# Clustered attention: second operand of odd heads, turn of the cluster scores and the place of the maxima

## Chip, cores and metric

The kernel runs on one core of one Trainium2 chip. The metric is device time in microseconds (us) of one execution; below 0.2% a difference counts as none.

## What is computed

The program is an attention in which a query only sees the keys of its own cluster, followed by two mixture layers. The change touches the attention alone:

```python
q_n = q / (norm(q) + 1e-06); k_n = ...; c_n = ...       # B=2, H=8, S=768, D=64, 16 clusters
q_assign = argmax(einsum('bhsd,hcd->bhsc', q_n, c_n), -1)
k_assign = argmax(einsum('bhsd,hcd->bhsc', k_n, c_n), -1)
mask = q_assign[:, :, :, None] == k_assign[:, :, None, :]
scores = where(mask, scale * q @ k.T, -1e9)
attn = softmax(scores) @ v
x = relu(attn_tokens @ w_in) ** 2 @ w_out               # first mixture layer
out = sum over e of p[:, e] * (relu(x @ w1[e]) @ w2[e]) # second
```

## The kernel before, in words

**Units.** There are 16 heads (batch by head) of six tiles of 128 queries, so 96 units. The loop over `g` (L1234) works on three units at once: it issues the score products of unit g+2 (`S`, L656) and their row maximum (`M`, L665), the exponential of unit g+1 (`E`, L676), the turns of unit g's probabilities (`T0`, `T1`, L689), which ScalarE rounds (`H0`, `H1`, L694) and VectorE completes by the rest (`L0`, `L1`, L695), and the products with v of the two units before (`P0`, `P1`, L703 and L705). Every large product takes its operands as a rounded part and a rest. The order of these steps is written out by hand in `ORDER`, a line for even and one for odd g, and each engine executes its own instructions in that order:

```python
"S T0 X1 M E T1 R Y1 H0 P0 X2 C H1 L0 L1 C K Y2".split(),        # even g
"S X1 E M T0 T1 Y1 H0 C P1 X2 R L0 H1 C L1 Y2 O K C".split()]    # odd g
```

`X1` and `X2` run the TensorE part of a queued job and `Y1`, `Y2` its way out of PSUM; `R` runs jobs that need no TensorE; `C` takes one entry from the queue `dq`, so that an even g takes up to two and an odd g up to three. An entry `None` only passes one turn of `C`.

**Preparing a pair of heads.** While earlier heads are worked on, the next pair j (heads 2j and 2j+1, first unit u0 = 12j) is prepared by jobs that are placed in units by `AT` and `START`. `trans_slot` (L393) turns q and k at u0-14 to u0-11; its way out writes the rounded part and the rest (`nkh`, `nkl`, `nqh`, `nql`, one buffer each) on GpSimd (L53, L402). `pair_scores` (L478) makes the cluster scores of both heads at u0-11 and u0-10, copied by ScalarE to `ys` (L484). `pair_turn` (L494) turns three 128x128 blocks of `ys` with the fp32 identity at u0-10 and u0-9, once for each half of the tokens; a column group holds, for each of four combinations, two parts of 16 scores, and VectorE adds the two parts on the way out (L499). `pair_ops` finds the first best cluster: `first` is a row maximum on VectorE (L535) and three operations on GpSimd (L524 to L526), `second` another maximum (L539) and four GpSimd operations (L529 to L532) that write the one-hot rows `oh`. `pair_hot` (L551) turns `oh` on TensorE at u0-5; ScalarE copies the result (L556), and `hot_rows` sends it by four DMAs (L568) into the last 16 rows of the operands `q2` and `k2`.

**Other jobs.** `stack` copies parts of the pair's q and k by DMA (L414, L416) into the operands of each head: part 0 makes `k1` (rounded part over rest), part 1 makes `k2`, `q1` and `q2`. For an odd head i they stand at 6i-10 and 6i-9; for the pair's numbering, at u0-4 and u0-3. `norm_steps` places the finishing of the pair that is two before: at u0-6 of the pair j its `f4` runs in `R`, two additions of 128x384 on GpSimd (L786), and at u0-5 `f5`, which multiplies and rounds (L740, L749).

Of the kernel before, what the change touches and what calls it, by code (L numbers as in the profile page):

```python
# [8 lines left out]
F32 = mybir.dt.float32  # L9
# [3 lines left out]
ALU = mybir.AluOpType  # L13
AX = mybir.AxisListType
# [11 lines left out]
    "S X1 E M T0 T1 Y1 H0 C P1 X2 R L0 H1 C L1 Y2 O K C".split()]  # L26
WARM = [11, 6, 4, 3, 1, 2]
START = {'t': [0, 0, 1], 'a': [3, 3, 4, 4, 7], 'stack1': 4, 'stack': 5, 'head': 2}
AT = {"stack1": (-11, -10), "stack": (-9, -9), "ohd": -7, "splitv": -3, "load": -10,
      "t": [-14, -13, -12, -11], "a": [-11, -10, -10, -9, -5], "conv": (8, 9, 10, 12, 13, 27), "pieces": 46,  # L30
      "norm": (11, 12, 16, 18, 19, 26), "in": (22, 34)}

# [2 lines left out]
def moe_attention_kernel(  # L35
# [13 lines left out]
    nc = tc.nc  # L49
# [5 lines left out]
    B, H, S, D = q.shape  # L55
    C = centroids.shape[1]
# [7 lines left out]
    HALF = S // 2  # L64
    QT = HALF // 128
# [5 lines left out]
    const = ctx.enter_context(tc.tile_pool(name="const", bufs=1))  # L71
# [5 lines left out]

    identf = const.tile([128, 128], F32, name="identf")
    identr = const.tile([128, 128], F32R, name="identr")
    zeros = const.tile([128, 1, 1], F32, name="zeros")  # L80
    wgt = const.tile([128, 1, C], F32, name="wgt")
    pe_p = const.tile([128, B * NTT, E], F32, name="pe_p")
# [131 lines left out]
    with tc.manual_schedule():  # L214
# [23 lines left out]
        ps_m = actx.enter_context(tc.tile_pool(name="ps_m", bufs=1, space=PSUM))  # L238
# [52 lines left out]
        for c in range(C):  # L291
            nc.gpsimd.memset(wgt[:, :, c:c + 1], float(C - c))
        nc.gpsimd.memset(cp.bitcast(F32), 0.0)
        ohs["first"] = as_p.tile([128, NTT, 2, 2, C], F32R, tag="oh", name="oh").rearrange(
            "p t e s c -> p (t e s c)")[:, 0:2 * NTT * C].rearrange("p (s t c) -> p s t c", t=NTT, s=2)

# [12 lines left out]
        vt, stk, kq = {}, {}, {}  # L309
        dq = []  # L310

        def step():
            f = dq.pop(0)
            if f:
                f()
# [90 lines left out]
        def stack(i, part):  # L406
            (kh, kl), (qh, ql) = kq[i // 2, "nk"], kq[i // 2, "nq"]
            r = slice(D * (i % 2), D * (i % 2) + D)
            for nm, rows, top, low in ((("k1", 128, kh, kl),),
                                       (("k2", D + C, kh, None), ("q1", 128, qh, qh),  # L410
                                        ("q2", D + C, ql, None)))[part]:
                t = stk[i, nm] = stk_p.tile(
                    [rows, S], F32R, tag=nm, name=nm, bufs=3 if nm == "k1" else 2)
                nc.sync.dma_start(out=t[0:D].bitcast(F32), in_=top[r].bitcast(F32))  # L414
                if low is not None:
                    nc.sync.dma_start(out=t[D:2 * D].bitcast(F32), in_=low[r].bitcast(F32))  # L416

# [70 lines left out]
        def pair_turn(j, half):  # L488

            def f():  # L490
                m = ps_m.tile([128, QT, 128], F32, tag="m", name="m")
                for t in range(QT):
                    c0 = half * HALF + t * 128
                    nc.tensor.transpose(m[:, t], ys[j][:, c0:c0 + 128], identf)  # L494

                def evac():
                    if half == 0:
                        ya[j] = as_p.tile([128, 4 * NTT, C], F32, tag="A", name="A")
                    nc.vector.reduce_sum(  # L499
                        out=ya[j][:, half * 4 * QT:(half + 1) * 4 * QT],  # L500
                        in_=m.rearrange("p t (g s c) -> p (t g) c s", g=4, s=2), axis=AX.X)
                    if half:
                        first, second = pair_ops(j, ya.pop(j))
                        if j == 1:
                            first()
                            dq.extend([None] * 3 + [second])
                        else:
                            dq.extend([None, first, None, None, None, second])
                return evac
            return f  # L510

        ys, ya = {}, {}

        def pair_ops(j, A):
            mx = as_p.tile([128, 4 * NTT, 1], F32, tag="mx", name="mx")
            mx2 = as_p.tile([128, 4 * NTT, 1], F32, tag="mx2", name="mx2")
            off = as_p.tile([128, NTT, 2, C], F32, tag="off", name="off")
            oh = ohs["p", j] = as_p.tile([128, NTT, 2, 2, C], F32R, tag="oh", name="oh")
            shp = [128, 4 * NTT, C]
            V, P = nc.vector, nc.gpsimd  # L520
            av = A.rearrange("p (t x e) c -> p t x e c", x=2, e=2)

            def p1():
                P.tensor_tensor(A, A, mx.to_broadcast(shp), op=ALU.subtract)  # L524
                P.tensor_scalar(A, A, 2.0 ** 63, 2.0 ** 63, op0=ALU.mult, op1=ALU.mult)
                P.tensor_tensor(A, A, wgt.to_broadcast(shp), op=ALU.add)  # L526

            def p2():
                P.tensor_tensor(A, A, mx2.to_broadcast(shp), op=ALU.subtract)  # L529
                P.tensor_scalar(oh[:, :, :, 0], av[:, :, 1], 0.0, -1.0, op0=ALU.min, op1=ALU.max)  # L530
                P.tensor_scalar(off, av[:, :, 0], 0.0, -1.0, op0=ALU.min, op1=ALU.max)
                P.tensor_scalar(oh[:, :, :, 1], off, 1.0, -NEG, op0=ALU.add, op1=ALU.mult)  # L532

            def first():
                V.reduce_max(out=mx, in_=A, axis=AX.X)  # L535
                p1()

            def second():
                V.reduce_max(out=mx2, in_=A, axis=AX.X)  # L539
                p2()  # L540
            return first, second

        def pair_hot(j):

            def f():
                while dq:
                    step()
                om = oms[j] = as_p.tile([128, HALF], F32R, tag="ohm", name="ohm")
                m = ps_m.tile([128, HALF], F32R, tag="m", name="m")
                for a in range(QT):  # L550
                    nc.tensor.transpose(  # L551
                        m[:, a * 128:(a + 1) * 128],
                        ohs["p", j][:, 2 * a:2 * a + 2].rearrange("p t e s c -> p (t e s c)"), identr)

                def evac():
                    nc.scalar.copy(om, m.bitcast(F32))  # L556
                    hot_rows(2 * j)
                return evac
            return f
# [3 lines left out]
        def hot_rows(i):  # L563
            j, e = divmod(i, 2)
            for s, t in ((0, 0), (1, 0), (1, 1), (0, 1)):
                nm = ("q2", "k2")[s]
                r = ((2 * t + e) * 2 + s) * C
                nc.sync.dma_start(  # L568
                    out=stk[i, nm][D:D + C].bitcast(F32).rearrange(
                        "c (a t n) -> c a t n", a=QT, t=2)[:, :, t],  # L570
                    in_=oms[j][r:r + C].bitcast(F32).rearrange("c (a n) -> c a n", a=QT))
# [180 lines left out]
        def norm_steps(hp):  # L752
# [36 lines left out]
            def f5(half):  # L789
                norm_scaled(hp, half, st["rb"][:, half * HALF:(half + 1) * HALF], nc.gpsimd, round_pool)  # L790

            u = 2 * hp * NTT
            at(early, u + AT["norm"][0], f1)
            at(slots, u + AT["norm"][1], f2)
            for f, x in ((f3, 2), (f4, 3), (lambda: f5(0), 4)):
                at(early, u + AT["norm"][x], f)
            at(early, u + (AT["norm"][4] + 1 if hp == NH // 2 - 2 else AT["norm"][5]), lambda: f5(1))

# [286 lines left out]
        second = [split64(0, 1, j, lambda shp, j=j: cv_p[j % 2](shp), nc.vector) for j in range(NF)]  # L1085
# [18 lines left out]
        def whole(f):  # L1104
# [20 lines left out]
            out=nrm, in0=nr2, scalar=ss, in1=nrm, op0=ALU.mult, op1=ALU.add)  # L1125
# [8 lines left out]
            out=cl, in0=c2, scalar=nrm, in1=ch.bitcast(F32), op0=ALU.mult, op1=ALU.subtract)  # L1134
# [11 lines left out]
        for e in range(2):  # L1146
            r = slice(D * e, D * e + D)
# [41 lines left out]
        def at(d, g, f):  # L1189
            d.setdefault(max(g, 0), []).append(f)  # L1190

        for i in range(1, NH):
            u0 = i * NTT
            if i > 1:
                for n, x in enumerate(("stack1", "stack")):
                    at(early, START[x] if i == 2 else u0 + AT[x][i % 2], lambda i=i, n=n: stack(i, n))
                if i % 2:
                    at(early, u0 + AT["ohd"], lambda i=i: hot_rows(i))
            at(early, u0 + AT["splitv"], lambda i=i: split_v(i))
# [291 lines left out]
        p, q, sums2, mix = conv_in(2)  # L1491
# [4 lines left out]
        op, oq = conv_out(2, [lambda shp: mp["c1"][:, 0], cv_p[1]])  # L1496
# [4 lines left out]
        for c in range(2, NC1 - 1):  # L1501
            p, q, sums2, mix = conv_in(c + 1)
            if c == 2:
                put(c, (0, 2, 2, 2, 7, 7, 7, 9, 9),
                    [p[0], p[2][0:1], q[0][0:3], p[2][1:2], q[0][3:5], q[1], sums2, mix[1], mix[0]])
                op, oq = conv_out(
                    3, [lambda shp: raw_t[1, 0, 1][:, 0:512], cv_p[1]])
# [5 lines left out]
            else:  # L1513
# [18 lines left out]
                op, oq = conv_out(c + 1)  # L1532
# [441 lines left out]
```

## Time and profile before

| | |
|---|---|
| three runs | 1001.54, 1002.58, 1003.63 us; median 1002.58 |
| profiled execution | 1001.82 us, of which the span from first to last instruction is 1000.0 |
| attention | from the start to some 225 us |
| pairs prepared in the loop | 7 (j = 1 to 7), six of them (j = 2 to 7) with `f4` of an earlier pair at u0-6 |
| granted TensorE clock | 0.999 |

The page of the profile gives busy times of the engines PE (TensorE products), PEld (its weight loads), DVE (VectorE), ACT (ScalarE), POOL (GpSimd) and of the queue SP, which issues the DMAs. Busy PE is an upper bound, since products overlap in its pipeline; what a product costs is read from the distance of its start to the next one's.

### The profile page before, as it was taken

To read this page: it belongs to the slowest core of one execution; us is meant where nothing else is said; L and a number is where in the kernel's file an instruction comes from. 1 tells how busy PE (TensorE), PEld (TensorE's weight loads), DVE (VectorE), ACT (ScalarE), POOL (GpSimd) and SP (SyncE) were. 2 spreads that over 40 slices of the span, in tenths; PEclk is the share of its full clock that TensorE was granted. 3 is DMA by queue.
4 is the path that set the end of the run, shared out by engine and by line. 5 is a ranking of instruction groups with operands and counts; after the bars stand their busy time and mean duration, and the time that the engine had idled before them with its cause. 6 is when DMAs were issued, how large, how long until landed. Compare 5 with 4: busy or idle time off the path is not lost.

```text
span 1000.0 us, 16363 instructions
## 1 busy us (share of the span) xinstructions
PE 988.3 (99%) x5889; PEld 905.4 (91%) x5889; DVE 787.2 (79%) x1210; ACT 574.3 (57%) x1139; POOL 609.7 (61%) x588
## 2 busy tenths in 40 slices
PE   8999999999999999999999999999999999999998
PEld 8999999999888888888889899898999899999997
DVE  6898989888899997987685555567666987887787
ACT  6888889988655644456454343444445445444442
POOL 6468777773326604346666767667688665666555
PEclk9999999999999999999999999999999999999999
DMA  7577876852112122211125454554527554334511
GB/s 187 128 155 182 208 165 157 194 136 79 42 43 81 47 85 85 69 58 65 41 64 199 158 212 179 179 201 168 205 99 248 176 190 168 115 127 161 190 43 64
DMA packets 92504, 133.78 MB, mean 134 GB/s; under 512 B 29876, under 2 KB 55368, under 8 KB 92424
## 3 DMA queue, kind: packets, MB, share of 16 engines
q1 hardware_dynamic: 92424, 132.74, 44.1%
q8 instruction: 46, 0.75, 0.3%
q14 instruction: 34, 0.28, 0.1%
HBM read 80.93 MB, written 28.88 MB: 110 GB/s over the span
## 4 chain that ended last, share of the span: by engine, by line
PE 90%; DVE 3%; POOL 2%; DMA 2%; ACT 1%; issue 1%; SPq 1%; POOLq 0%; ACTq 0%
PE bank L900 27%; PE bank L1062 13%; PE bank L931 13%; PE bank L1852 10%; PE s L656 6%; PE t L689 6%; PE bank L878 5%; PE po L703 3%; PE po L705 3%; PE s L878 1%; PE m L478 1%; DMA raw<-in_moe_w_dram 1%; POOL wzl L1770 1%; PE m L393 1%; PE po L1099 1%
## 5 line engine op out<-in xcount | busy, mean ns | idle before, releaser
L695 DVE TENSOR_TENSOR ptl<-t,pth 128x384 fp32r<-128x384 f32 x192 | 98.2, 550 | 20.3 <-ACT pth L694 19.9
L900 PE MATMUL bank<-xa,wxh 128*128 128x384 f32 (+1 forms) x392 | 103.9, 346 | 2.0 <-DVE x L1827 1.8
L665 DVE TENSOR_REDUCE nb<-s 128x1 f32<-128x768 f32 x96 | 91.1, 950 | 7.8 <-PE s L656 7.4
L1078 DVE SCALAR_TENSOR_TENSOR x<-bank,pe_p,x 128x512 f32<-128x512 f32 x90 | 67.5, 751 | 35.7 <-PE bank L1062 35.7
L1861 DVE SCALAR_TENSOR_TENSOR x<-bank,pe_p,x 128x256 f32<-128x256 f32 x156 | 70.3, 478 | 27.3 <-PE bank L1852 26.2
L1006 POOL TENSOR_TENSOR wxl<-raw,wxh 128x512 fp32r<-128x512 f32 (+1 forms) x36 | 47.1, 1328 | 70.1 <-ACT wxh L1005 70.1
L694 ACT CAST pth<-t 128x384 fp32r<-128x384 f32 x192 | 84.0, 487 | 9.0 <-PE t L689 8.2
L900 PE MATMUL bank<-xa,wyh 128*128 128x384 f32 (+1 forms) x344 | 88.7, 338 | 0.0
L676 ACT ACTIVATE p<-s,nb 128x768 f32<-128x768 f32 x96 | 88.1, 917 | 0.3 <-DVE nb L665 0.2
L656 PE MATMUL s<-k,q 80*128 80x384 f32 (+1 forms) x384 | 86.2, 345 | 0.1
L689 PE MATMUL t<-identf,p 128*128 128x128 f32 x576 | 85.4, 276 | 0.4 <-DVE ptl L695 0.3
L703 PE MATMUL po<-pth,vv 128*128 128x256 f32 x288 | 80.4, 309 | 0.0
L931 PE MATMUL bank<-gb,wzh 128*128 128x512 f32 x240 | 78.0, 391 | 0.2
L900 PEld LDWEIGHTS bank<-xa,wxh 128*128 128x128 f32 x392 | 71.3, 188 | 7.0 <-DVE x L1827 2.6
L689 PEld LDWEIGHTS t<-identf,p 128*128 128x128 f32 x576 | 67.6, 140 | 9.5 <-DVE ptl L695 6.8
L1770 POOL TENSOR_TENSOR wzl<-raw,wzh 128x512 fp32r<-128x512 f32 x32 | 55.2, 1736 | 31.0 <-ACT wzh L1767 31.0
L705 PE MATMUL po<-ptl,vv 128*128 128x256 f32 x288 | 72.5, 281 | 0.0
L900 PE MATMUL bank<-rt,wyh 128*128 128x384 f32 (+1 forms) x264 | 71.0, 350 | 0.0
L900 PE MATMUL bank<-xa,wxl 128*128 128x384 f32 (+1 forms) x196 | 67.7, 345 | 0.0
L207 ACT CAST wyh<-raw 128x512 fp32r<-128x512 f32 x36 | 22.3, 622 | 78.6 <-POOL raw L200 61.3
L656 PEld LDWEIGHTS s<-k,q 80*128 80x128 f32 (+1 forms) x384 | 63.4, 189 | 0.5 <-ACT p L676 0.2
L900 PEld LDWEIGHTS bank<-xa,wyh 128*128 128x128 f32 x344 | 62.0, 188 | 1.4
(355 smaller groups left out, 2978.6 us busy)
## 6 DMA issues: line engine op xcount, KB each, us to landing
raw<-in_moe_w_dram SPq DMA_DIRECT2D x34, 512.0 KB, 4.7
raw<-in_moe_w_dram SPq DMA_DIRECT2D x8, 1024.0 KB, 7.6
raw<-in_moe_w_in_dram SPq DMA_DIRECT2D x7, 1024.0 KB, 5.3
kept<-wyh SPq DMA_DIRECT2D x14, 512.0 KB
kept<-wyl SPq DMA_DIRECT2D x14, 512.0 KB, 2.7
wyh<-kept SPq DMA_DIRECT2D x13, 512.0 KB, 4.7
wyl<-kept SPq DMA_DIRECT2D x13, 512.0 KB, 5.3
raw<-in_moe_w_out_dram SPq DMA_DIRECT2D x6, 1024.0 KB
```

Of the source, the lines that this page charges most:

```text
L656: nc.tensor.matmul(s[:, j, 0:HALF], stk[i, nq][:, t * 128:(t + 1) * 128], stk[i, nk][:, j * HALF:(j + 1) * HALF], start=first, stop=not first)
L665: nc.vector.tensor_reduce(out=nb, in_=s_ps[u][:, :, 0:HALF], axis=AX.XY, op=ALU.max, negate=True)
L676: nc.scalar.activation(p, s_ps.pop(u)[:, :, 0:HALF], AF.Exp, bias=nb_t.pop(u), accum_out=sums_t[hp][:, i % 2, t:t + 1])
L689: nc.tensor.transpose(tp[:, j], p_sb[u][:, half, j * 128:(j + 1) * 128], identf)
L694: return (lambda: nc.scalar.copy(dh, tp), lambda: nc.vector.tensor_tensor(dl, tp, dh.bitcast(F32), op=ALU.subtract))
L695: lambda: nc.vector.tensor_tensor(dl, tp, dh.bitcast(F32), op=ALU.subtract))
L703: nc.tensor.matmul(po_t[pr], vt[i][:, kt], pth[:, kt], start=(kt == 0), stop=False)
L705: nc.tensor.matmul(po_t[pr], vt[i][:, kt], ptl[:, kt], start=False, stop=(kt == NTT - 1))
L900: nc.tensor.matmul(ps, w[:, ks], x(xx)[:, kt], start=(first and kt == 0 and z == 0), stop=(kt == 1 and z == 2), skip_group_check=True)
L931: nc.tensor.matmul(o, a[:, d], b, start=(ft == 0 and z == 0), stop=(ft == 1 and z == 2))
L1062: nc.tensor.matmul(o, a, w[:, f, cols], start=(f == 0 and z == 0), stop=(f == 1 and z == 2))
L1852: nc.tensor.matmul(o, a, w, start=(i in (1, 5, 2) and f == 0 and z == 0), stop=(f == 1 and z == 2), skip_group_check=True)
```

## The change

Five edits. `fold`, 128x64, is made once on GpSimd as the sum of two column groups of the identity. `pair_turn` multiplies `ys` by `fold` in fp32 in place of turning it by the identity: 64 output columns in place of 128, and the two parts come out added, so that VectorE copies 128x192 in place of adding 128x384 down to it. For j > 1, `first` and `second` come one entry of `dq` later. For odd heads `k1` is sent two units earlier, and `k2` copies from the upper half of `k1` (the same values) in place of from `nkh`. The way out of `pair_hot` is split: ScalarE copies half the columns and VectorE the other half.

```diff
-AT = {"stack1": (-11, -10), "stack": (-9, -9), ...
+AT = {"stack1": (-11, -12), "stack": (-9, -9), ...
+    fold = const.tile([128, 4, C], F32, name="fold")
+        idf = identf.rearrange("p (g s c) -> p g s c", g=4, s=2)
+        nc.gpsimd.tensor_tensor(fold, idf[:, :, 0], idf[:, :, 1], op=ALU.add)
...
         def stack(i, part):
+            k2 = stk[i, "k1"][0:D] if part and i % 2 else kh[r]
...
-                nc.sync.dma_start(out=t[0:D].bitcast(F32), in_=top[r].bitcast(F32))
+                nc.sync.dma_start(
+                    out=t[0:D].bitcast(F32), in_=(k2 if nm == "k2" else top[r]).bitcast(F32))
...
         def pair_turn(j, half):
-                m = ps_m.tile([128, QT, 128], F32, tag="m", name="m")
+                m = ps_m.tile([128, 4 * QT, C], F32, tag="m", name="m")
                 for t in range(QT):
                     c0 = half * HALF + t * 128
-                    nc.tensor.transpose(m[:, t], ys[j][:, c0:c0 + 128], identf)
+                    nc.tensor.matmul(
+                        m[:, 4 * t:4 * t + 4], ys[j][:, c0:c0 + 128], fold, start=True, stop=True)
...
-                    nc.vector.reduce_sum(
-                        out=ya[j][:, half * 4 * QT:(half + 1) * 4 * QT],
-                        in_=m.rearrange("p t (g s c) -> p (t g) c s", g=4, s=2), axis=AX.X)
+                    nc.vector.tensor_copy(ya[j][:, half * 4 * QT:(half + 1) * 4 * QT], m)
...
-                            dq.extend([None, first, None, None, None, second])
+                            dq.extend([None, None, first, None, None, None, second])
...
         def pair_hot(j):
-                    nc.scalar.copy(om, m.bitcast(F32))
+                    c0 = HALF // 2
+                    nc.scalar.copy(om[:, 0:c0], m[:, 0:c0].bitcast(F32))
+                    nc.vector.tensor_copy(om[:, c0:], m[:, c0:].bitcast(F32))
```

## Rows read from the trace of the kernel before

**Rows 1.** The page: busy time, share of the span and instructions of each engine
```profile
PE 988.3 (99%) x5889; PEld 905.4 (91%) x5889; DVE 787.2 (79%) x1210; ACT 574.3 (57%) x1139; POOL 609.7 (61%) x588
```
**Rows 2.** Chain that ended last, 195 to 222 us: start us, us, what
```profile
by line: PE s L656 30.9%; PE t L689 28.7%; PE po L703 15.0%; PE po L705 14.9%; PE m L478 5.2%; PE m L393 2.4%; PE m L494 2.4%; PE m L551 0.8%; PE m L765 0.4%
...
202.84 0.12 PE po L703
...
203.56 0.33 PE m L494 x3
...
209.06 0.98 PE t L689 x6
...
211.47 0.66 PE t L689 x6
...
214.91 0.21 PE m L551 x3
```
**Rows 3.** Line L494: its instructions, duration ns min/median/max
```profile
L494 PE MATMUL m<-identf,ys x42: 270/272/308, 28.9 to 206.0; 128*128 128x128 f32 x42
```
**Rows 4.** Timeline of the weight loads, 8.8 to 10.4 us: start us, us
```profile
9.00 0.75 PEld L420 LDWEIGHTS m<-cc,k 128*128 128x128 f32 x6
9.66 0.75 PEld L420 LDWEIGHTS m<-cc,q 128*128 128x128 f32 x6
```
**Rows 5.** Timeline of DVE, pair 7, 206 to 212 us
```profile
206.64 0.55 DVE L499 TENSOR_REDUCE A<-m 128x192 f32<-128x384 f32 x1
...
207.97 0.54 DVE L535 TENSOR_REDUCE mx<-A 128x24 f32<-128x384 f32 x1
208.43 1.01 DVE L695 TENSOR_TENSOR ptl<-t,pth 128x384 fp32r<-128x384 f32 x2
...
211.17 0.55 DVE L539 TENSOR_REDUCE mx<-A 128x24 f32<-128x384 f32 x1
```
**Rows 6.** Line L1141: a DVE copy out of PSUM, duration ns
```profile
L1141 DVE CAST cc<-m x1: 425/425/425, 8.2 to 8.2; 128x256 fp32r<-128x256 f32 x1
```
**Rows 7.** Timeline of POOL, pair 7, 208 to 215 us, idle before in brackets
```profile
208.59 0.84 POOL L524 TENSOR_TENSOR A<-A,mx 128x384 f32<-128x384 f32 x1 [3.13 <-DVE mx L535]
...
211.80 0.84 POOL L529 TENSOR_TENSOR A<-A,mx 128x384 f32<-128x384 f32 x1 [0.67 <-DVE mx L539]
...
213.47 0.35 POOL L532 TENSOR_SCALAR oh<-off 128x192 fp32r<-128x192 f32 x1
213.91 1.98 POOL L786 TENSOR_TENSOR xs<-xs,xm 128x384 f32<-128x384 f32 x2
```
**Rows 8.** Timeline of PE, pair 7, the turns of the one-hot rows
```profile
214.74 0.37 PE L551 MATMUL m<-identr,oh 128*128 128x128 f32 x3
```
**Rows 9.** The same two ends in pair 4: timelines of POOL and PE
```profile
124.81 0.59 POOL L532 TENSOR_SCALAR oh<-off 128x192 fp32r<-128x192 f32 x1
...
126.08 0.37 PE L551 MATMUL m<-identr,oh 128*128 128x128 f32 x3
```
**Rows 10.** Who waited for whom, 20 to 225 us: total us, times, longest us
```profile
POOL nkh L53 <- DMA k<-nkh: 15.2, 4, 4.9
```
**Rows 11.** Timeline of PE at the cluster scores of pairs 4 and 5
```profile
110.76 0.33 PE L478 MATMUL m<-nqh,cp 128*128 128x384 f32 x1
111.52 0.45 PE L478 MATMUL m<-nql,cp 128*128 128x384 f32 x1 [0.42 <-POOL nql L402]
...
141.80 0.44 PE L478 MATMUL m<-nql,cp 128*128 128x384 f32 x1 [0.64 <-POOL nql L402]
```
**Rows 12.** Timelines of ACT and POOL: the first copy of pair 4's k, and its rounding
```profile
102.23 0.49 ACT L400 ACTIVATE kqf<-m 128x384 f32<-128x384 f32 x1
...
106.27 0.51 POOL L53 TENSOR_SCALAR nkh<-kqf 128x384 fp32r<-128x384 f32 x1 [4.61 <-DMA k<-nkh]
```
**Rows 13.** Line L414, the copies of `stack`: from issue to landing
```profile
DMA to landing us min/median/max: 2.5/3.5/6.3
```
**Rows 14.** Timeline of POOL in the first 25 us: its first work on loaded data
```profile
8.78 0.66 POOL L53 TENSOR_SCALAR cp<-cc 64x128 fp32r<-64x128 f32 x2 [6.26 <-DVE cc L1141]
```

More of the change, by code (lines that the diff above doesn't have):

```diff
@@ L28 @@
 START = {'t': [0, 0, 1], 'a': [3, 3, 4, 4, 7], 'stack1': 4, 'stack': 5, 'head': 2}
-AT = {"stack1": (-11, -10), "stack": (-9, -9), "ohd": -7, "splitv": -3, "load": -10,
+AT = {"stack1": (-11, -12), "stack": (-9, -9), "ohd": -7, "splitv": -3, "load": -10,
       "t": [-14, -13, -12, -11], "a": [-11, -10, -10, -9, -5], "conv": (8, 9, 10, 12, 13, 27), "pieces": 46,
```

## The prediction

> **What bounds the kernel now.** I read the busy shares first: TensorE is busy for 99% of the span, VectorE for 79%, GpSimd for 61% [rows 1]. A busy TensorE may overlap with itself, so the next view is the chain that ended last, in the last stretch of the attention: every line of it is TensorE's, two thirds of it the score products, the turns of the probabilities and the products with v [rows 2]. So TensorE's own instructions and its waits set the attention's end, and what the change does to other engines counts where TensorE comes to wait for them. Such waits stand in two places. In the unit after the first maximum, six turns of L689 take 0.98 us instead of 0.66 [rows 2]: VectorE starts the rests L695 of the unit before only when the maximum L535 is through [rows 5], and these free the bank that the next turn writes. And in pairs 4 and 5 the cluster scores wait for the rest of q from GpSimd [rows 11].
>
> **The fp32 product in place of the turn.** Now three turns take 0.33 us of the chain [rows 2], 0.11 each, and there are 42 in 14 blocks [rows 3]. A product's weights are the 128 columns of `ys`, its moving operand 64 columns of `fold`. No fp32 product that isn't a turn stands in the trace. The nearest row for short products under a load of 128 columns is L420: six loads of products of 32 columns take from 9.00 to 9.66 us, 0.11 each, so there the load sets the pace [rows 4]. That is one load for a rounded operand. An fp32 operand that goes through the array as a high and a low part would need two, 0.22 a product and 0.66 a block: 0.33 more than the turns, 14 x 0.33 = 4.6 us. Below, a product could be as quick as a turn of rounded data, L551 with 0.21 a block [rows 2]: 14 x -0.12 = -1.7. Above, four parts with a load each cost 0.44 a product, 14 x 0.99 = +13.9. I take 0.22, since the work is fp32 times fp32 and L420's pace is set by its load, as this one's must be.
>
> The Trainium skill (page FP8 and Floating Point Precision, section TensorE Precision Notes) says that a true fp32 product goes through the array in four passes. No row of this kernel shows an fp32 product that isn't a turn, so the trace neither bears it out nor speaks against it. Read as four streams over one load, it would make the sum 1009.2 where L420's pace makes it 1013.4; it is rival A below.
>
> **VectorE.** The sum of halves L499 takes 0.55 us [rows 5]; in its place comes a copy of 192 columns out of PSUM. L1141 copies 256 columns out of PSUM in 425 ns [rows 6]; the copy takes between 425 x 192/256 = 319 and 425, say 0.36. Two a pair give back 0.38, the half copy in `pair_hot` takes 0.36 of it again, so in sum nothing. The half copy stands behind L695 in unit u0-5, while TensorE is at its turns; it has no cost on the chain, and without that cover 7 x 0.36 = 2.5 us at most. ScalarE is rid of half of L556; it is not on the chain, so nothing.
>
> **The maxima later.** This is the largest term, and it is one of order. Before, `dq` is [None, first, None, None, None, second] when the second turn's way out runs at the end of unit u0-9; by the turns of `C` that ORDER has, `first` falls to the first `C` of u0-8 and `second` to the last `C` of u0-7. The trace agrees: L535 stands ahead of the two L695 of that unit, L539 behind those of the next [rows 5]. With one entry more, `first` falls to the second `C` of u0-8, behind L0 and L1, and `second` to the first `C` of u0-6. On VectorE that is behind M of u0-6, and on GpSimd it is behind `R` of u0-6, where `f4` issues its two additions L786. Before, GpSimd did L524 to L526, L529 to L532, then L786 [rows 7]; now it does L524 to L526, L786, L529 to L532. And the one-hot turns L551 at u0-5 need L532.
>
> In times of pair 7: the maximum's place, 0.46 (207.97 to 208.43), goes from ahead of L695, and the copy saves 0.19, so the two L695 start not at 208.43 but at 207.78. Two take 1.01, and the maximum begins at some 208.7 and ends at 209.24, where it was 208.51 [rows 5]. GpSimd follows 0.08 later, and L524 to L526 take from 208.59 to 211.13 (211.80 less 0.67 idle), 2.54: until 211.86. L786 takes 0.08 + 1.98: 213.92. L529 to L532 take from 211.80 to 213.82, 2.02, with 0.08 ahead: 216.02 [rows 7]. The second maximum is done well before that and binds nothing. TensorE came to L551 at 214.74 [rows 8], so it ends up 1.3 us later than before. The 0.32 that L689 no longer waits lies inside this: TensorE reaches L551 at 214.42 and waits 1.6. If the product is dearer, L551 and the maximum (which follows M, which follows the scores behind the product) shift alike, and the 1.3 stands. In pair 4 L532 ended at 125.40, 0.68 ahead of L551, where in pair 7 it was 0.92 [rows 7 to 9]; pairs 3 and 5 look like 4, pairs 2 and 6 like 7, so three pairs have 1.3 and three 1.5: 8.4 us. Pair 1 keeps its order and has no `f4`: nothing. Behind L551 stand the score products of the next unit, so nothing makes the time up; the four DMAs of `hot_rows` follow L551 at the same distance as before. Bounds: L786's 2.06 less the 0.67 of idle time that it fills, with the maximum not later at all, less the slack 0.92 or 0.68, gives 0.5 to 0.7 a pair, 3.6 us; a maximum later by the full 1.01 gives 9.6.
>
> **k1 earlier, k2 from k1.** GpSimd waited 15.2 us in four waits for copies out of `nkh` to end [rows 10]. In pair 4 the data was copied by 102.72 and rounded from 106.27 [rows 12]. The last reader of `nkh` becomes k1's copy, issued at u0-6, three units of some 2.4 us (209.06 to 211.47) ahead of where k2's stood; such copies land in 6.3 us at most [rows 2, 13], so this wait goes, and k2's wait for k1 costs SP nothing. On TensorE it is worth the two late products: in pair 4 it starts 0.76 after the product ahead of it (110.76 to 111.52) and 0.42 of that shows as idle, in pair 5 0.64 is idle [rows 11]. Idle time alone is 1.06, and as products overlap the loss is more; I take -1.4. What is late next is the copies out of `nqh` and `nql`, which stay where they were; bounds 0 and -1.4. The two DMAs of k1 pass the four of `hot_rows` on SP; that queue only waits there.
>
> **fold.** One GpSimd operation of 64 columns while that engine idles 6.26 us for the centroids [rows 14]: nothing, and some 0.3 us if that cover were gone.
>
> **Sum.** 4.6 + 8.4 - 1.4 = +11.6 us. The profiled execution took 1001.82 (span 1000.0), 0.76 under the median of 1002.58; the sum gives 1013.4 on the one, 1014.2 on the other. I say 1013.5.
>
> **The rivals.** *A: a cheap product.* If one load serves four streams of 64 columns, a product is like one of 256 columns, L703, 0.12 [rows 2], and a block 0.36: 14 x 0.03 = 0.4 us, in all 1001.8 + 0.4 + 8.4 - 1.4 = 1009.2. For it speaks that rounded operands need one load [rows 4]; against it that it is not known whether fp32 weights do. The Trainium skill's four passes, cited above, read in the plainest way, are this case.
>
> *B: a dear product*, four loads: 1001.8 + 13.9 + 8.4 - 1.4 = 1022.7.
>
> *C: faster, since the one-hot turns are not late.* Place: GpSimd between L535 and L551. If the second maximum's four operations still end before TensorE comes to L551, the 8.4 goes, the 6 x 0.32 = 1.9 of L689's waits and the 1.4 come back, and with A's product it is 1001.8 + 0.4 - 1.9 - 1.4 = 998.9. It decides where L532 ends no more than 0.92 (pair 7) or 0.68 (pair 4) later than before. GpSimd's idle 3.13 and 0.67 ahead of L524 and L529 [rows 7] speak for room; against it, 3.13 lies before the maximum and L786 alone is 2.06.
>
> *D: no change:* C's order with the product at 0.22: 1001.8 + 4.6 - 3.3 = 1003.1.
>
> *E: the change of `k2` doesn't free GpSimd*, because the copies out of `nqh` and `nql` bind as well: 1001.8 + 4.6 + 8.4 = 1014.8.
>
> **How the numbers follow.** Forecast 0.52, A 0.17, B 0.10, C 0.11, D 0.06, E 0.04. A measurement of this kernel tells 0.2% from no change, 2 us: faster is C, 0.11; no change D, 0.06; slower the rest, 0.83. The range leaves out most of C and D and the worst of B. Its lower end is A's product with the small bound of the wait and the 1.4: 1001.8 + 0.4 + 3.6 - 1.4 = 1004.4, say 1005. The upper end has a product of 0.33 (two loads, and two streams that don't hide behind them), 14 x 0.66 = 9.2, and 9.6 for the wait: 1020.6, say 1021.
>
> **What would show it.** Right: L551's weight load waits for L532 on GpSimd, 1.3 to 1.6 us in six pairs; L786 stands between L526 and L529; L494's products start some 0.22 apart; the wait of `nkh` for a DMA and the idle time ahead of `nql` are gone, and L689 after the first maximum takes 0.66. Wrong: L551 without a wait (C or D), L494 at 0.12 (A) or 0.44 (B) apart, or a new wait elsewhere on TensorE of over 1 us a pair.

## The result, and the profile after

The changed kernel took 1013.64 us (median of 4 runs, 1012.28 to 1014.34), the kernel before 1002.56 beside it (4 runs): ratio 1.0112, 95% interval 1.01 to 1.0124, so 11.1 us slower. The forecast was 1013.5. The profiled executions, on which the sum was worked out, took 1012.28 and 1001.82 (spans 1010.2 and 1000.0), a difference of 10.5 where the sum had 11.6. In a part of the executions TensorE's granted clock is at 0.5, its lower level of 1.2 GHz, for 3.4 us near 780 us, far behind the attention (781.4 to 784.8 in the trace of the first experiment), and the runs with a mean clock of 0.998 take some 1 to 2 us longer than those of the same kernel at 1.0, so that a median of few runs is no finer than that.

The attention itself goes on beyond the 225 us given above: in the kernel before the score products of its last unit start at 242.4. What has ended by 225 is the preparation of the pairs.

The changed kernel's lines are 3 to 6 higher: `T` is L695 and its rest L701, the product with fold L499, its copy L505, the maxima L539 and L543, their GpSimd operations L528 to L530 and L533 to L536, the one-hot turns L555, `f4` L792, the sum in `norm_steps` L765.

The chain that ended last, 200 to 232 us of the changed kernel, pieces in order of time (start us, us, what), answers to [rows 2]:

```profile
215.14 0.61 PE m L499 x6
...
216.51 0.34 PE t L695 x3
216.88 0.49 ACT pth L700
217.43 1.01 DVE ptl L701 x2
218.44 0.47 DVE mx L539
218.97 0.85 POOL A L528
219.90 0.51 POOL A L529
220.50 1.01 POOL A L530
221.50 1.93 POOL xs L792 x2
223.43 0.81 POOL A L533
...
225.06 0.36 POOL oh L536
225.47 0.45 PE m L555 x3
```

Where every step was TensorE's, the chain now leaves it for 8.6 us (216.88 to 225.47): over ScalarE's and VectorE's halves of a turn to the first maximum, then through seven GpSimd operations with the two additions of `f4` in the middle, and back to TensorE at the one-hot turns. The same stretch in GpSimd's timeline, with idle time ahead in brackets, answers to [rows 7]:

```profile
218.97 0.84 POOL L528 TENSOR_TENSOR A<-A,mx 128x384 f32<-128x384 f32 x1 [4.90 <-DVE mx L539]
...
221.45 1.98 POOL L792 TENSOR_TENSOR xs<-xs,xm 128x384 f32<-128x384 f32 x2
223.38 0.86 POOL L533 TENSOR_TENSOR A<-A,mx 128x384 f32<-128x384 f32 x1
...
225.06 0.35 POOL L536 TENSOR_SCALAR oh<-off 128x192 fp32r<-128x192 f32 x1
```

L533 no longer waits for the second maximum; it waits for L792. On TensorE the last product with v starts at 224.06, and then the timeline shows a hole (compare [rows 8]):

```profile
221.85 0.86 PE L662 MATMUL s<-k,q 128*128 128x384 f32 x4
222.62 1.01 PE L695 MATMUL t<-identf,p 128*128 128x128 f32 x6
...
224.06 0.28 PE L711 MATMUL po<-ptl,vv 128*128 128x256 f32 x1
225.47 0.45 PE L555 MATMUL m<-identr,oh 128*128 128x128 f32 x3 [1.13 <-POOL oh L536]
225.76 0.41 PE L662 MATMUL s<-k,q 128*128 128x384 f32 x1
```

The same unit in the kernel before:

```profile
212.67 0.86 PE L656 MATMUL s<-k,q 128*128 128x384 f32 x4
213.38 0.82 PE L689 MATMUL t<-identf,p 128*128 128x128 f32 x6
...
214.62 0.28 PE L705 MATMUL po<-ptl,vv 128*128 128x256 f32 x1
...
214.95 0.94 PE L656 MATMUL s<-k,q 128*128 128x384 f32 x4
```

From these score products to the next unit's it takes 3.91 us in place of 2.28. The hole is 1.29 of the difference: the one-hot turns start 1.41 behind the last product with v, in the kernel before 0.12. The other 0.34 are the turns L695, which now wait for VectorE behind the second maximum. In return, the turns behind the first maximum no longer wait, and that unit is 0.32 shorter.

Who waited for whom, 20 to 235 us (total us, times, longest us):

```profile
POOL nkh L53 <- ACT kqf L403: 19.4, 12, 5.0
...
PEld m L555 <- POOL oh L536: 8.5, 6, 1.5
...
PE m L555 <- POOL oh L536: 7.3, 6, 1.3
```

Six waits at L555, as forecast, and GpSimd's `nkh` no longer waits for a DMA [rows 10 before] but for its data.

The product, by line L499 (duration ns min/median/max) and in TensorE's timeline:

```profile
L499 PE MATMUL m<-fold,ys x84: 217/275/275, 28.4 to 215.5; 128*128 128x64 f32 x84
```

```profile
212.12 0.28 PE L711 MATMUL po<-ptl,vv 128*128 128x256 f32 x1
212.25 0.78 PE L499 MATMUL m<-fold,ys 128*128 128x64 f32 x6
212.83 0.94 PE L662 MATMUL s<-k,q 128*128 128x384 f32 x4
```

The 42 products are recorded as 84, six a block: each is two products with a load each. From the start of L711 to the next score product takes 0.71 us; the kernel before took 0.37 (from 203.28 to 203.65):

```profile
203.28 0.28 PE L705 MATMUL po<-ptl,vv 128*128 128x256 f32 x1
203.40 0.49 PE L494 MATMUL m<-identf,ys 128*128 128x128 f32 x3
203.65 0.96 PE L656 MATMUL s<-k,q 128*128 128x384 f32 x4
```

That is 0.34 more a block and, if all were like this one, 4.8 us in 14.

### The profile page after: what moved, and what is told of

The parts are those of the page before. It is cut to its first block, busy times and chain, and to the rows that moved or that the text cites. A ratio compares the mean times of both kernels' runs of the same rounds, so it can differ in the third digit from the quotient of the medians.

```text
span 1010.2 us, 16477 instructions
## 1 busy us (share of the span) xinstructions
PE 992.3 (98%) x5931; PEld 909.6 (90%) x5931; DVE 790.1 (78%) x1217; ACT 573.5 (57%) x1139; POOL 608.4 (60%) x589
## 4 chain that ended last, share of the span: by engine, by line
PE 71%; DVE 15%; POOL 6%; ACT 3%; issue 2%; DMA 2%; SPq 0%; POOLq 0%; ACTq 0%; DVEq 0%
PE bank L906 24%; PE bank L1068 13%; PE bank L1858 10%; PE bank L937 6%; PE s L662 5%; PE t L695 4%; PE po L709 2%; PE po L711 2%; DVE x L943 2%; DVE ptl L701 1%; PE bank L884 1%; DVE fa L178 1%; PE m L483 1%; POOL xs L792 1%; DVE fa L173 1%
## 5 line engine op out<-in xcount | busy, mean ns | idle before, releaser
L701 DVE TENSOR_TENSOR ptl<-t,pth 128x384 fp32r<-128x384 f32 x192 | 98.0, 549 | 17.1 <-ACT pth L700 16.4
L695 PE MATMUL t<-identf,p 128*128 128x128 f32 x576 | 84.5, 275 | 0.7 <-DVE ptl L701 0.3
L695 PEld LDWEIGHTS t<-identf,p 128*128 128x128 f32 x576 | 67.7, 140 | 9.1 <-DVE ptl L701 5.5
L711 PE MATMUL po<-ptl,vv 128*128 128x256 f32 x288 | 72.5, 281 | 0.0
```

The lines of the kernel that those rows point to most:

```text
L695: nc.tensor.transpose(tp[:, j], p_sb[u][:, half, j * 128:(j + 1) * 128], identf)
L701: lambda: nc.vector.tensor_tensor(dl, tp, dh.bitcast(F32), op=ALU.subtract))
L711: nc.tensor.matmul(po_t[pr], vt[i][:, kt], ptl[:, kt], start=False, stop=(kt == NTT - 1))
```

## The experiments

The forecast is a sum of three terms that could be right by chance. The first four runs put single edits on the kernel before, or take one away from the changed kernel; the split of the copy in `pair_hot` is only parted from the rest by the last two.

**The order of the maxima, taken out of the change.**

```diff
-dq.extend([None, None, first, None, None, None, second])
+dq.extend([None, first, None, None, None, second])        # on the changed kernel
```

> The changed kernel with the queue of before ([None, first, None, None, None, second]), all other edits kept. Theory (the wait of the one-hot turns comes from the place of the second maximum behind f4): the six waits of 1.1 to 1.3 us ahead of L555 go, about 8 us, so 1005 us. Rival (the waits come from GpSimd's load by the earlier k1 and k2, or from the product): they stay, 1012 to 1014 us.

1004.55 us against 1002.7, ratio 1.0021 (1.0011 to 1.0031), 9.1 us less than the changed kernel; no wait of L555 for GpSimd is left in the list of waits. The rival falls: k1, k2 and the product are all still there.

**The order alone**, the same line changed the other way on the kernel before.

> The kernel before with one more None in the queue and nothing else. Theory: one-hot turns late by 1.3 to 1.7 us in six pairs, less the wait of L689 that moves, so +8 to +10: 1011 to 1012 us. Rival (it needs the product or the k2 edit as well): 1002 to 1004 us.

1011.41 us, ratio 1.0093 (1.0079 to 1.0107), +8.7. The waits are those of the changed kernel:

```profile
PEld m L551 <- POOL oh L532: 8.6, 6, 1.5
PE m L551 <- POOL oh L532: 7.3, 6, 1.3
```

So one `None` in a list carries four fifths of the loss, without any of the other edits.

**The product alone.**

```diff
-nc.tensor.transpose(m[:, t], ys[j][:, c0:c0 + 128], identf)
+nc.tensor.matmul(m[:, 4 * t:4 * t + 4], ys[j][:, c0:c0 + 128], fold, start=True, stop=True)
-nc.vector.reduce_sum(...)
+nc.vector.tensor_copy(ya[j][:, half * 4 * QT:(half + 1) * 4 * QT], m)
```

> The kernel before with the fp32 product by fold and VectorE's copy, nothing else. Theory: 14 blocks of 0.61 in place of 0.33 us on the chain, +3.9, less up to 1.9 that the turns L689 no longer wait for the maximum since TensorE comes later: 1004.5 to 1006.5 us. Rival (VectorE's shorter evacuation pays for the product): 1001 to 1003 us.

1007.78 us, ratio 1.0053 (1.0039 to 1.0067), +5.1, above the expected 2 to 4. The cost of the products is there. The return from L689 was overrated: where up to 1.9 us was expected, the units behind the first maximum are only 0.05 to 0.08 shorter in six pairs. And the wait for the rest of q at the cluster scores has grown (to three waits of TensorE with 1.5 us in all, where [rows 11] show two).

**k1 earlier and k2 from k1, alone.**

```diff
-AT = {"stack1": (-11, -10), ...
+AT = {"stack1": (-11, -12), ...
-in_=top[r].bitcast(F32)
+in_=(k2 if nm == "k2" else top[r]).bitcast(F32)     # k2 = stk[i, "k1"][0:D] for odd i
```

> The kernel before with k1 of odd heads two units earlier and k2 from k1, nothing else. Theory: GpSimd's four waits for the copies out of nkh go, and with them the waits for nql in pairs 4 and 5: -1.4, 1001.2 us. Rival (the copies out of nqh and nql hold the same chain up): 1002.6 us, with the idle time ahead of L478 as before.

1001.92 us, ratio 0.9996 (0.9988 to 1.0005): no difference is shown, and the profiled span is 1000.0 as before. Yet the edit did what it was made for: no wait of TensorE for `nql` is in the list any more. What came in its place is in the timelines of VectorE, GpSimd and the weight loads of this kernel, in the unit (one ahead of a pair's first) where `norm_steps` adds 1e-9 to the row sums (its L697 is the rest of a turn):

```profile
194.81 0.84 DVE L761 TENSOR_SCALAR r<-sums 128x12 f32<-128x12 f32 x1
195.56 0.55 DVE L697 TENSOR_TENSOR ptl<-t,pth 128x384 fp32r<-128x384 f32 x1
```

```profile
194.61 1.01 POOL L402 TENSOR_TENSOR nkl<-kqf,nkh 128x384 fp32r<-128x384 f32 x1
```

```profile
196.16 0.31 PEld L691 LDWEIGHTS t<-identf,p 128*128 128x128 f32 x3 [0.26 <-DVE ptl L697]
```

An operation on 12 columns takes 0.84 us; it ends 0.03 after GpSimd's L402 does (195.65 against 195.62). The turn behind it then waits. Over all seven pairs, the kernel before and this one:

```profile
L759 DVE TENSOR_SCALAR r<-sums x7: 161/164/233, 47.3 to 223.7; 128x12 f32<-128x12 f32 x7
```

```profile
L761 DVE TENSOR_SCALAR r<-sums x7: 164/575/844, 47.6 to 223.9; 128x12 f32<-128x12 f32 x7
```

In the kernel before, L402 was not yet running at that time, because GpSimd had been kept waiting by the DMA that the edit gets rid of. The second four runs test this, and the two larger terms more closely.

**The changed kernel with `f4` behind the second maximum.** The later maxima stay; GpSimd's order is again L533 to L536, then L792.

```diff
-"norm": (11, 12, 16, 18, 19, 26)
+"norm": (11, 12, 16, 19, 19, 26)
```

> The changed kernel with f4 one unit later (u0-5 in place of u0-6), so that its two additions stand behind the second maximum's four operations on GpSimd again; the later maxima stay. Theory (the wait is the place of L786 in GpSimd's order): 2.06 us less ahead of the one-hot turns, the six waits of 1.1 to 1.3 us shrink to 0.2 or less, 1005 to 1006.5 us. Rival (the maxima as such are too late): the waits keep over 0.7 us, 1010 us or more.

1005.46 us, ratio to the kernel before 1.0032 (1.0019 to 1.0044), 8.2 less than the changed kernel. The waits at L555 shrink to three of 0.2 at most:

```profile
PEld m L555 <- POOL oh L536: 0.7, 3, 0.2
```

So it is the place of two additions in GpSimd's order that costs. That the maxima come later costs little by itself: with `f4` moved back, the unit of the one-hot turns is still 0.41 to 0.53 us longer than in the kernel before, where it was 1.63 to 1.82. The same move of `f4` on the kernel with the later maxima alone:

> The kernel before with one more None and f4 one unit later, nothing else. Theory: the one-hot turns wait some 0.3 us in a pair, and L689's 0.3 after the first maximum goes in return: 1002 to 1004 us, where the None alone gave 1011.4. Rival: over 1007.

1003.76 us, ratio 1.0007 (0.9999 to 1.0016), where the None alone gave 1011.41: within the noise of the kernel before. The trace is finer: from the first unit's score products to the last unit's, the attention is 2.35 us longer than before, with the None alone 9.79.

**Without the addition on VectorE.** The 1e-9 is left out; a row's sum is at least 1.

```diff
 # on the kernel before with k1 earlier and k2 from k1
-lambda: nc.vector.tensor_scalar(r, sm, 1e-9, None, op0=ALU.add),
-lambda: nc.vector.reciprocal(r, r),
+None,
+lambda: nc.vector.reciprocal(r, sm),
```

> The kernel before with k1 earlier and k2 from k1, and without the addition of 1e-9 to the row sums in norm_steps (the reciprocal reads the sums; a sum holds an exponential of 0, so it is at least 1). Theory: with the k2 edit that VectorE operation of 12 columns falls beside a GpSimd operation with two inputs and lasts 0.57 to 0.85 us in six pairs in place of 0.16 to 0.23, and the turns behind it wait 0.19 to 0.25; without it these waits go: 1.2 us less than with the k2 edit alone, 1000.6 us. Rival (the reciprocal that takes its place is held up alike, or the wait comes from the earlier GpSimd work in another way): the waits ahead of L689 stay, 1001.9 us.

1000.08 us, ratio 0.9975 (0.9966 to 0.9985): 3.0 us under the kernel before (1003.05 beside it), and 1.8 under the edit alone (1002.7 beside that); by the traces the attention is 1.3 shorter than with the edit alone, and 1.2 shorter than in the kernel before. The waits of L691 in that unit are gone, and the reciprocal, which now falls beside the same GpSimd operation (here at 193.6 us), isn't held up:

```profile
193.63 0.22 DVE L762 RECIPROCAL r<-sums 128x12 f32<-128x12 f32 x1
```

```profile
192.97 1.01 POOL L402 TENSOR_TENSOR nkl<-kqf,nkh 128x384 fp32r<-128x384 f32 x1
```

**The product with twice the columns**, on the kernel with the product alone: `fold` put in twice, 128 output columns, the copy of the first 64 of each.

> The kernel before with the product by fold alone, fold's 64 columns put in twice (128 output columns, the second half unused). Theory (two loads of 128 columns set the pace of a product): six passes a block start 0.10 us apart as with 64 columns, and the time is that of the product alone, 1007 to 1009 us. Rival (the streamed columns set it): twice the distance, +0.6 us a block, 1015 to 1017 us.

1007.4 us, ratio 1.0048 (1.0033 to 1.0064), as with 64 columns. Six products of 128 columns take from 210.39 to 210.98, 0.59 us; of 64 columns in the kernel with the product alone, from 208.26 to 208.85, the same:

```profile
210.39 0.83 PE L498 MATMUL m<-fold,ys 128*128 128x128 f32 x6
210.98 0.96 PE L661 MATMUL s<-k,q 128*128 128x384 f32 x4
```

```profile
208.26 0.78 PE L497 MATMUL m<-fold,ys 128*128 128x64 f32 x6
208.85 0.94 PE L658 MATMUL s<-k,q 128*128 128x384 f32 x4
```

The streamed columns don't set the pace up to 128. That the loads do fits the two loads recorded for each product; a product with fewer weight columns, which would show it, wasn't run.

**A version that beats both.** Two runs keep the k1 and k2 edit and the whole computation, and give the addition to ScalarE; the second also splits the way out of `pair_hot`, as the change does.

```diff
-lambda: nc.vector.tensor_scalar(r, sm, 1e-9, None, op0=ALU.add),
+lambda: nc.scalar.activation(r, sm, AF.Copy, bias=1e-9),
```

> The kernel before with k1 earlier and k2 from k1, and the addition of 1e-9 done by ScalarE in place of VectorE; nothing is left out. Theory (the addition on VectorE is what GpSimd holds up): the waits of L689 in the unit of the reciprocal stay away, 1000 to 1001 us, faster than both kernels. Rival (it was the queue's length on VectorE): ScalarE's operation of some 0.2 us costs as much, 1002 us.

> The same with the way out of pair_hot split between ScalarE and VectorE as in the change. Theory: the split is off the chain but for the last pair, whose first score products wait some 0.5 us for the rows that hot_rows sends: 999.5 to 1001 us, within 0.5 us of the other. Rival (VectorE's half copy holds up the turns): 1 us or more slower than the other.

1000.24 us, ratio 0.9981 (0.9972 to 0.999), and 1000.28, ratio 0.9976 (0.9965 to 0.9987), beside 1002.42 for the kernel before: both some 2 us faster than it, which is at the 0.2% that counts here, and 13 faster than the changed kernel, with nothing left out.

The two medians are the same, but the traces are not. Who waited for whom, first without the split and then with it:

```profile
PEld t L691 <- DVE ptl L697: 6.3, 31, 0.6
```

```profile
PEld t L693 <- DVE ptl L699: 4.1, 17, 0.6
```

ScalarE's copy of `pair_hot` takes 0.48 us without the split and 0.32 with it (125.31 and 124.28 us, pair 4). Without the split ScalarE has no idle time from there to its next roundings L696 (126.83 us). VectorE's rests follow the roundings, and the next six turns wait for the rests and take 1.01 us (from 127.97); with the split they take 0.86 (from 126.92).

That unit is 0.15 to 0.17 us shorter in each of the seven pairs, 1.1 in all, and from the first unit's score products to the last's the two attentions are 1.2 and 2.6 us shorter than in the kernel before. So the split is worth a good microsecond, which the medians of these runs hide.

## Why the prediction was right, and where it wasn't

**The order of the maxima** was forecast at +8.4 and is worth +8.7 alone and 9.1 when taken out of the change (9.8 and 7.8 by the traces of the attention). Its mechanism holds link by link, but for one: L792 stands between L530 and L533, L555 waits in six pairs, and moving `f4` back alone all but ends the waits. From the end of the first maximum (218.89) to the end of L536 (225.41) it took 6.5 us, where the working by pair 7 had 6.8 (209.24 to 216.02). The split into three pairs of 1.3 and three of 1.5 came out too: pairs 3 to 5 have a hole of 1.47, the others 1.29. The link that differs: TensorE was to come to the one-hot turns 0.32 earlier and to wait 1.6 in pair 7. It does save that 0.32 behind the first maximum, but loses it again behind the second, and waits 1.3; the net is the same. Rivals C and D, which needed the one-hot turns on time, are out. (The upper bound of 9.6 doesn't follow from its own working: a maximum later by 1.01 in place of 0.73 adds 0.28 in six pairs to 8.4, which is 10.1.)

**The product** was forecast at +4.6, from two loads at L420's pace, and shows 0.32 to 0.34 a block, 4.6 in all; alone it cost 5.1. The profile records two products with a load each for every fp32 product, 0.10 apart, and twice the columns cost nothing. Rival A's 0.12 and B's 0.44 a product are out: it is 0.20. Both parts of the difference were taken 0.07 to 0.08 too large: by starts a block is 0.59 and not 0.66, and the three turns that it replaces 0.25 and not 0.33. The four passes that the Trainium skill gives a true fp32 product (page FP8 and Floating Point Precision, section TensorE Precision Notes), read as four streams over one load, would have been A; the trace shows two weight loads, and time that doesn't grow from 64 to 128 columns.

**VectorE's copy** was put at 0.36 and takes 0.356:

```profile
L505 DVE COPY A<-m x14: 345/356/358, 29.2 to 215.8; 128x192 f32<-128x192 f32 x14
```

That this pays for little of the product was right: with the product alone, the units behind the first maximum get 0.05 to 0.08 us shorter in six pairs and 0.36 in pair 1.

**k1 and k2: this step failed.** The forecast was that the DMA's wait goes, which it did, and that -1.4 comes of it, with "what is late next is the copies out of `nqh` and `nql`". The late products of pairs 4 and 5 give back even more, 1.9. But late next was something else, which the sum doesn't have: with GpSimd no longer waiting, its L402 falls beside VectorE's addition of 1e-9, which is held until L402 ends, and the turns behind it come late; that unit is 0.23 to 0.31 longer in six pairs, 1.6 us in all. So the edit alone shows no gain (ratio 0.9996).

**The split of `pair_hot`'s copy: this step failed too.** It was put at nothing: of ScalarE the prediction says "it is not on the chain, so nothing". It is worth 1.1 us, as the last two runs show: ScalarE's roundings come before the rests that the turns of one unit in each pair wait for.

**The total: its last microseconds are luck.** The distance from one unit's first score product to the next one's can be compared over the whole attention. It is the same in both kernels, to 0.02 us, but for these places (changed kernel less kernel before, us):

| | forecast | traces |
|---|---|---|
| the product, 14 blocks | +4.6 | +4.6 |
| the order of the maxima, six pairs | +8.4 | +8.4 |
| late products of pairs 4 and 5 | -1.4 | -1.9 |
| turns behind VectorE's addition, six pairs | not seen | +1.6 |
| the split copy, seven pairs | 0 | -1.1 |
| a unit in pair 1 (-0.4) and one in the last pair (+0.2) | not seen | -0.2 |
| sum | +11.6 | +11.4 |

The two large terms are right, and by their mechanism. That the total is right to a few tenths is luck: a cost of 1.6 that wasn't seen stands against three gains of 1.8 in all that weren't either. The profiled spans differ by 10.2 and not by 11.4; the other -1.2 lies ahead of the attention's first score products and behind its last ones, and no run parts it.

**Not settled:** why VectorE's addition is held and its reciprocal isn't, and whether the loads or something else of a fixed length set an fp32 product's pace.

## What to carry to other kernels

Where engines execute in program order, moving a step by one place in a hand-written queue moves it past whatever another list issues in between; write out every engine's order on both sides before pricing it. An engine that stands idle waiting for a DMA may be keeping out of another's way: ask, when such a wait is removed, what will run beside what. Price an fp32 product by its two recorded passes with a load each, not by its columns, when the columns are few (here 64 and 128 cost the same). And where terms of a microsecond have to be told apart, compare the starts of a repeated instruction in both traces: the medians here hid a gain that the traces show in every pair.

## What was not expected of the hardware

A VectorE `tensor_scalar` from and to SBUF on 12 fp32 columns, 0.16 us by itself, took 0.57 to 0.85 when a GpSimd `tensor_tensor` with two inputs of 384 columns was running, and ended 0.03 after it. Beside a GpSimd operation with one input (L53, at 166.0 and 195.2 us of the kernel before) it took 0.23 and again ended 0.03 after it. A VectorE `reciprocal` of the same 12 columns beside the same operation took 0.21 to 0.22, as without it. The Trainium skill (page GPSIMD Engine Reference, section 8. Key points) says that GpSimd shares its SBUF interfaces with VectorE and that the two contend when VectorE's instruction is in a 2-port mode or has two SBUF inputs. The runs agree that one operation is held up and another of the same size isn't; which mode either was in no run here shows. Here the hold lasted to the end of GpSimd's instruction.
